# A state-space layer and a SoLU block on one Trainium2 core: one pair of accumulator banks for two products, and whole 64x64 blocks stored to memory instead of their 32x32 diagonal blocks

## The chip, the cores and the metric

The kernel runs on one core of one Trainium2 chip. The metric is the device time of one execution in microseconds (us), taken as the median of several executions. The engines are named as in the profile: PE (matmuls; PEld is its weight load), DVE (vector), ACT (activations), POOL (GpSimd) and SP (here it only issues DMAs). Every engine works through its own list of instructions in order. A "q" behind an engine's name is its sequencer.

## The reference, cut to what matters

The first part is a recurrence over 768 steps for 4 batches of 8 heads with a 40x40 state; its output, regrouped to 3072 rows of 320, goes through a feed-forward block:

```python
for t in range(S):                     # r, k, v, w, a, b: (4, 8, 768, 40)
    y[:, :, t] = einsum('bhd,bhde->bhe', r_t, state)
    Sa = einsum('bhde,bhe->bhd', state, a_t)
    state = state * w_t[:, :, None, :] - einsum('bhd,bhe->bhde', Sa, b_t) \
            + einsum('bhd,bhe->bhde', v_t, k_t)
x = y.transpose(0, 2, 1, 3).reshape(3072, 320)
h = x @ w_in                           # 320 x 1024
solu = h * softmax(h)
ln = (solu - mean(solu)) / sqrt(var(solu) + 1e-6) * g_ln
out = ln @ w_out                       # 1024 x 320
```

## The kernel before, in words

**Tiling.** The 768 steps are cut into 12 chunks of 64. A work item `i` is one chunk of one pair of batches, so there are 24 items. Within a chunk the recurrence becomes matmuls on 64x64 blocks, one for each of the 16 (batch, head) couples of the item, plus the inverse of a unit triangular 64x64 matrix for each couple. That matrix is called `nt` and is made by `norm(i)`: 16 matmuls into the accumulator tile `pnt`, and a masked copy by DVE (`masked`, line 383).

**The inverse.** The two 32x32 diagonal blocks of each `nt` are inverted column by column on DVE (`invert`, lines 427 to 451, tiles `blk`, `prod`, `uu`). DVE needs them in another layout: 128 partitions, one 32x32 block each, for two items at once (`GRP = 2`). So `norm` stores them to a DRAM tile `nt_dram`, and `spread` loads them back as `blk`, in four DMAs of 32 partitions, as soon as both items' stores have landed. The inverses go through DRAM again (`uu_dram`) and come back with `bring` as `tu` and `uh`. The off-diagonal 32x32 part is made on PE from products: `couple` (tile `py`, read by ACT into `wy`, line 481) and `close` (tile `pz`).

**Slots.** The main loop (line 827) runs over slots `i` from -1 to 27, and is a software pipeline written out by hand. In slot `i` stand, in PE's order: `solved(i)` (tile `pu`), `scores(i+1)` (`ps`), `stated(i)` (transposes of the state, `pst`; in the slots named in `THIN`, line 28, ahead of `scores`), transposes for item `i+5` (`front`, `front_b`, `decay_turned`), parts of the feed-forward block of earlier items (`hidden`, tile `h`; `output`, tile `po`, in two halves of four accumulating steps), then `couple(i+1)` (`py`), `norm(i+5)` (`pnt`), `answered(i)` (`pl`, line 591, read by DVE into `lu`), the second half of `output`, `close(i+1)` (`pz`), `read(i)` (`pyo`), `carried` and `driven` (`px`), `folded` (`plnT`), and transposes for item `i+2`. `norm(i+5)` exists up to slot 18 only, since there are 24 items; `couple(i+1)` exists up to slot 22. The first four `norm`s (items 0 to 3) stand in a loop ahead of the slots (line 771).

Between PE's pieces DVE works off the inverse in small steps (`some(n)` runs the next `n` steps; `shares`, line 825, says how many at each place of a slot). `flip(i+1)` (line 469, `tu<-tu`) is a DVE transposition that `couple(i+1)` needs.

**Accumulator banks.** The pool `ps1` gives pairs of banks with the tag `banks` and two buffers:

```python
def banks(name):
    return ps1.tile([P, 2, 512], FP32, tag="banks", name=name)
```

Each call takes the buffer of the call before the last one, and the first matmul into it waits until that earlier tile has been read. In a full slot the calls come in the order `pu`, `ps`, `py`, `pnt`, `pl`, `pz`, `pyo`, `px`, so that `pl` takes the pair of `py`.

**Queues.** `norm(i)` stores with four DMAs of 32 partitions each (line 414), all on POOL for `i > 3`; for the first four items two of the four are on SP. POOL's list has also the products `kb` (`scaled`, line 345), part of the transposed outputs (`left`, tile `xT`), the loads `raw_r`, and `blk`.

Of the kernel before, what the change touches and what calls it, by code (L numbers as in the profile page):

```python
# [9 lines left out]
FP32 = mybir.dt.float32  # L10
# [8 lines left out]
C = 64  # L19
Q = 32  # L20
IN_ROWS = (((0, 80), (240, 280), (160, 168)), ((80, 160), (280, 320), (200, 208)), ((168, 200), (208, 240)))
GRP = 2
# [29 lines left out]
def kernel(  # L52
# [18 lines left out]
    nc = tc.nc  # L71
    B, H, S, D = r.shape
# [13 lines left out]
    dram = ctx.enter_context(tc.tile_pool(name="dram", bufs=3, space=bass.MemoryType.DRAM))  # L86
# [12 lines left out]
    def c_(name):  # L99
        lo, hi = where[name]  # L100
        return cst[:, lo:hi]
# [20 lines left out]
    for x in ex_t:  # L122
# [10 lines left out]
                          in_=c_("eye_hi").unsqueeze(1).to_broadcast([P, 8, Q]))  # L133
# [5 lines left out]
    def banks(name):  # L139
        return ps1.tile([P, 2, 512], FP32, tag="banks", name=name)  # L140

    def bank(name):
        return ps3.tile([P, 512], FP32, tag="bank", name=name)
# [83 lines left out]
    def mean_part(t, lo, hi, start, stop=True):  # L227
        for c in range(lo, hi):
            nc.tensor.matmul(t[:, 0:DM], lhsT=c_("mean"), rhs=w2[:, c, :], start=start and c == lo, stop=stop and c == hi - 1)

    def mean_of(lo, hi, begun):
        t = bank("pmean")
        nc.tensor.matmul(t[:, 0:DM], lhsT=ident, rhs=begun, start=True, stop=False)
        mean_part(t, lo, hi, False)
        return mean_kept(t)

    def mean_kept(t):
        mean = two.tile([P, DM], FP32, tag="osb", name="mean", bufs=1)
        nc.scalar.copy(out=mean, in_=t[:, 0:DM])
        return mean  # L240
# [7 lines left out]
    def half(p):  # L248
        return slice(C * p, C * p + C)

    def rows(p):
        return slice(C * p, C * p + D)
# [3 lines left out]
    def in_turn(tile_of, some=units):  # L256

        lots = {}
        for u in some:
            lots.setdefault(tile_of(*u), []).append(u)  # L260
        lots = list(lots.values())
        return [lot[n] for n in range(max(map(len, lots))) for lot in lots if n < len(lot)]

    def mm(o, lhsT, rhs, start=True, stop=True):
        nc.tensor.matmul(o, lhsT=lhsT, rhs=rhs, start=start, stop=stop, skip_group_check=True)  # L265
# [3 lines left out]
    def fence():  # L269
        nc.tensor.drain()  # L270
# [8 lines left out]
    st = [dict() for _ in range(N + 16)]  # L279
    blocks, inverse = {}, {}  # L280
# [10 lines left out]
    def ok(i):  # L291
        return 0 <= i < N
# [12 lines left out]
    def load_values(i):  # L305
        if not ok(i):
            return
        d = st[i]
        d["lv"] = two.tile([P, H, W2], FP32, tag="lv", name="lv", bufs=3)
        d["raw_r"] = two.tile([P, H, D], FP32, tag="raw_r", name="raw_r")  # L310
        load(d["lv"][:, :, C:], v, i)
        load(d["raw_r"], r, i, nc.gpsimd)
# [41 lines left out]
    def tokens(name, bufs=1):  # L354
        return two.tile([P, 2, 4, C], FP32, tag=name, name=name, bufs=bufs)
# [20 lines left out]
    def front_b(i):  # L376
        if not ok(i):
            return
        d = st[i]
        d["bT"] = kept("bT", turned("b", d["kb"][:, H:]))  # L380

    def masked(dst, t):
        nc.vector.tensor_tensor(out=dst, in0=t.rearrange("p b (j c) -> p b j c", j=4),  # L383
                                in1=tri.unsqueeze(1).unsqueeze(1).to_broadcast([P, 2, 4, C]), op=ALU.mult)

    def keyed(t, u):
        p, q, g, h = u
        return t[rows(h), p, 2 * q + g]

    def valued(t, u):  # L390
        p, q, g, h = u
        return t[rows(q), p, 2 * g + h]

    def norm(i):
        if not ok(i):
            return
        d = st[i]
        t = banks("pnt")
        for u in in_turn(lambda p, q, g, h: (h, p ^ h)):
            p, q, g, h = u  # L400
            j = 2 * q + g
            mm(t[half(p ^ h), h, j * C:j * C + C], keyed(d["bT"], u), keyed(d["aT"], u))
        nt = d["nt"] = tokens("nt", AHEAD)
        masked(nt, t[:, :, 0:256])
        n, at = divmod(i, GRP)
        if at == 0:
            blocks[n] = dram.tile([2, 2 * GRP * H, Q, Q], FP32, tag="nt_dram", name="nt_dram")

        to = blocks[n].rearrange("e (a h x) s c -> a e x s h c", a=GRP, x=2)[at]
        for x in range(2):  # L410
            for e in range(2):
                home = C * x + Q * e
                queue = nc.gpsimd if i > 3 or x else nc.sync
                queue.dma_start(out=to[e, x], in_=nt[home:home + Q].rearrange("p h j c -> p (h j) c")[:, :, Q * e:Q * e + Q])  # L414

    def spread(n):
        nb = two.tile([P, Q, Q], FP32, tag="blk", name="blk")
        for y in range(2):  # L420
            for e in range(2):
                home = C * y + Q * e
                queue = nc.gpsimd if n or y else nc.sync
                queue.dma_start(out=nb[home:home + Q], in_=blocks[n][e])
        return nb

    def invert(n):
# [43 lines left out]
    def couple(i):  # L471
        if not ok(i):
            return
        d = st[i]
        t = banks("py")
        for u in in_turn(lambda p, q, g, h: (p ^ h, p)):
            p, q, g, h = u
            j = 2 * q + g
            x = half(p ^ h)
            mm(t[half(p), h, j * Q:j * Q + Q], d["nt"][x, h, j], d["tu"][x, 4 * h + j, 0:Q])  # L480
        nc.scalar.activation(out=wy[:, :, :, 0:Q], in_=t[:, :, 0:4 * Q].rearrange("p h (j c) -> p h j c", j=4),  # L481
                             func=AF.Copy, scale=c_("neg_hi"))
# [104 lines left out]
    def answered(i):  # L587
        if not ok(i):
            return
        d = st[i]  # L590
        t = banks("pl")
        for u in in_turn(lambda p, q, g, h: (q, p)):
            p, q, g, h = u
            at = (2 * g + h) * C
            mm(t[half(p), q, at:at + C], d["nuT"][rows(q), p ^ h ^ q, 2 * h + g], valued(d["rT"], u))
        masked(d["lu"].rearrange("p (q x) c -> p q x c", q=2)[:, :, :, 0:C], t[:, :, 0:256])
# [230 lines left out]
    for i in range(-1, N + 3 + LAG):  # L827
        j, m = i + AHEAD, i - LAG
        pieces = shares.get(i, (0, 5, 4, 4) if i % GRP else (3, 5, 4, 5))
        some_weights = narrowed.get(i, (0, 0, 0))  # L830
        if i >= 1:
            bring(i + 1)
        if i >= 0:
            load_values(i + 2)
        narrow(0, pieces[0])

        solved(i)
        if i in THIN:
            stated(i)
            front(j)  # L840
        if i >= 0:
            scores(i + 1)
        if i >= 0:
            load_keys(j + 3, "w")
        load_keys(j + 2, "bak")

        if i not in THIN:
            stated(i)
            front(j)
        hidden(m - 2, ((0, 1),))  # L850
        if i == 3 + LAG:
            centred(mean)
        narrow(some_weights[1], pieces[1])
        front_b(j)
        if ok(j + 2):
            logged(j + 2)
        if i == 1 + LAG:
            first = ps2.tile([P, DFF], FP32, tag="h", name="mean")
            mean_part(first, 0, 2, True, False)
        decay_turned(j + 1)  # L860
        hidden(m - 2, ((1, 1),))
        flip(i + 1)
        highest(m - 2)
        scaled(j + 1)
        left(i - 1)
        if i == 1 + LAG:
            mean_part(first, 2, 3, False)
            mean = mean_kept(first)
        decay(j + 2)
        output(m - 3, 0)  # L870

        some(pieces[2])
        if i == 2 + LAG:
            mean = mean_of(3, 6, mean)
        couple(i + 1)
        exped(m - 2)
        norm(j)
        answered(i)
        weighed(m - 2)
        spreadof(m - 2)  # L880
        if ok(j) and j % GRP == GRP - 1:
            begin_inverse(j // GRP)
        if i == 0:
            turn_g()
        output(m - 3, 1)

        close(i + 1)
        read(i, True)
        carried(i + 1)
        narrow(some_weights[2], pieces[3], ok(j) and j % GRP == GRP - 1)  # L890
        by_value(i + 2)
        if ok(m - 1):
            hidden(m - 1, ((2, 0), (2, 1)))
        fence()
        read(i, False)
        driven(i + 1)
        leave(i)
        begin_narrow(narrowed.get(i + 1, (0,))[0])
        folded(m - 2)
        hidden(m - 1, ((0, 0),))  # L900
        attend_kv(i + 2)
        hidden(m - 1, ((1, 0),))
        attend_r(i + 2)
        if i == 2 + LAG:
            mean = mean_of(6, NF, mean)
# [30 lines left out]
```

## Time and profile before

| what | value |
|---|---|
| three runs | 621.02, 621.37 and 622.67 us; median 621.37 |
| the profiled execution | 622.67 us, of which the span of instructions is 620.9 |
| PE, DVE, ACT, POOL busy | 556.5, 450.2, 265.5, 279.1 us |
| mean granted clock of PE | 0.915 |
| `nt_dram` stores | 96 DMAs of 32 KB, 88 of them on POOL |
| `blk` loads | 48 DMAs of 128 KB, 46 of them on POOL |

The table is read from the profile's page and from the list of DMA issues. Times below are places in the span, counted from its start. "Idle before" an instruction is the time that its engine stood still ahead of it, with the instruction that ended it.

### The profile page before, as it was taken

The numbers are of one execution on the slowest core, as the hardware profiler recorded it, in microseconds if no ns is written. First come the engines' busy times: TensorE is split into PE (matmuls) and PEld (weight loads), VectorE is DVE, ScalarE is ACT, GpSimd is POOL, SyncE is SP. The second block draws the span as 40 slices with busy tenths as digits, with TensorE's granted clock in tenths as the row PEclk, the third lists the DMA queues.
The fourth block names the chain that finished last, engine by engine and source line by source line (L and its number), as shares of the span: only waits on it lengthen the run. The fifth ranks groups of instructions, "written<-read, shape, count | busy, mean of one in ns | idle before, by whom it ended". The sixth has DMA issues, their size and how long they took to land.

```text
span 620.9 us, 26739 instructions
## 1 busy us (share of the span) xinstructions
PE 556.5 (90%) x11453; PEld 404.8 (65%) x11453; DVE 450.2 (73%) x1262; ACT 265.5 (43%) x548; POOL 279.1 (45%) x492
## 2 busy tenths in 40 slices
PE   4662767979899999999999999999999999999994
PEld 3442655856677777777777777777777776776553
DVE  4696896988996878869868868868687688433431
ACT  3531454546444444444454454445434343443221
POOL 3455345365635654464574456265633721322200
PEclk9555755669999999999999999999999999999998
DMA  8774867365246455454554464464522612310000
GB/s 165 123 141 99 190 125 150 85 136 117 51 71 136 76 118 99 91 110 86 93 116 86 83 130 83 95 122 75 112 47 54 111 37 45 70 36 25 26 22 21
DMA packets 211150, 56.79 MB, mean 91 GB/s; under 512 B 196176, under 2 KB 206008, under 8 KB 211032
## 3 DMA queue, kind: packets, MB, share of 16 engines
q1 hardware_dynamic: 191544, 32.99, 30.3%
q0 software_dynamic: 12784, 17.42, 12.2%
q10 hardware_dynamic: 6704, 4.67, 2.7%
q8 instruction: 90, 1.47, 1.0%
q14 instruction: 28, 0.23, 0.1%
HBM read 40.10 MB, written 10.22 MB: 81 GB/s over the span
## 4 chain that ended last, share of the span: by engine, by line
PE 70%; DVE 14%; issue 5%; DMA 4%; POOL 4%; ACT 2%; ACTq 0%; DVEq 0%; POOLq 0%; SPq 0%
PE po L735 16%; PE h L265 16%; PE pyo L265 7%; DVE uu L442 4%; DVE prod L440 4%; PE plnT L724 4%; PE pu L265 3%; PE px L265 3%; PE ps L265 3%; PE py L265 2%; PE pl L265 2%; PE pz L265 2%; PE pst L517 2%; PE pcum L333 1%; PE pk L350 1%
## 5 line engine op out<-in xcount | busy, mean ns | idle before, releaser
L265 PE MATMUL h<-w_in,xT 128*128 128x512 f32 (+1 forms) x288 | 124.3, 618 | 0.0
L414 POOL DMA_DIRECT2D nt_dram<-nt x88 | 51.9, 597 | 142.6 <-DVE nt L383 130.6
L735 PE MATMUL po<-w,lnT 128*128 128x320 f32 x384 | 112.7, 438 | 0.5 <-ACT lnT L725 0.5
L442 DVE TENSOR_TENSOR uu<-uu,prod 128x30 f32<-128x30 f32 (+4 forms) x360 | 103.6, 288 | 12.3
L440 DVE TENSOR_TENSOR prod<-blk,uu 128x30 f32<-128x30 f32 (+4 forms) x360 | 97.1, 270 | 11.0 <-DMA blk<-nt_dram 1.4
L735 PEld LDWEIGHTS po<-w,lnT 128*128 128x128 f32 x384 | 71.0, 190 | 32.7 <-issue 4.1
L383 DVE TENSOR_TENSOR psi<-ps,cst 128x512 f32<-128x512 f32 x24 | 16.6, 690 | 57.2 <-PE ps L265 57.2
L713 POOL TENSOR_TENSOR rs<-c,mhalf 128x1 f32<-128x1 f32 x24 | 13.5, 563 | 90.3 <-DVE c L712 90.3
L662 POOL DMA_DIRECT2D xT<-x x96 | 49.8, 522 | 0.0
L265 PEld LDWEIGHTS h<-w_in,xT 128*128 128x128 f32 (+1 forms) x288 | 37.6, 190 | 9.5 <-issue 8.1
L682 DVE TENSOR_REDUCE nmax<-h 128x1 f32<-128x1024 f32 x24 | 28.6, 1193 | 18.6 <-PE h L265 18.6
L265 PE MATMUL pyo<-lv,kb 64*64 64x104 f32 x768 | 38.6, 272 | 2.2
L650 POOL TENSOR_TENSOR st<-tot,ex 104x160 f32<-104x160 f32 x44 | 21.7, 508 | 38.0 <-DVE tot L646 28.0
L265 PEld LDWEIGHTS pyo<-lv,kb 64*64 64x64 f32 x768 | 24.2, 144 | 21.7 <-issue 21.5
L265 PE MATMUL pyo<-lu,kb 64*64 64x104 f32 x768 | 37.3, 265 | 0.0
L481 ACT ACTIVATE wy<-py,cst 128x256 f32<-128x256 f32 x24 | 11.4, 474 | 54.9 <-PE py L265 54.9
L566 ACT COPY x<-px 128x320 f32<-128x320 f32 x24 | 10.2, 426 | 57.3 <-PE px L265 57.3
L288 POOL DMA_DIRECT2D raw_r<-in_r_dram x48 | 34.3, 719 | 0.0
L739 ACT ACTIVATE osb<-po,rs 128x320 f32<-128x320 f32 x24 | 12.7, 528 | 48.5 <-PE po L735 32.8
L690 ACT ACTIVATE e<-h,nmax 128x1024 f32<-128x1024 f32 x24 | 26.6, 1108 | 14.3 <-DVE nmax L682 14.3
L696 DVE TENSOR_TENSOR e<-h,e 128x1024 f32<-128x1024 f32 x24 | 29.2, 1217 | 4.7 <-ACT e L690 4.7
L704 DVE BATCH_NORM_STATS2 bs<-e 128x6 f32<-128x512 f32 x48 | 30.9, 686 | 0.8
(131 smaller groups left out, 1169.5 us busy)
## 6 DMA issues: line engine op xcount, KB each, us to landing
blk<-nt_dram POOLq DMA_DIRECT2D x46, 128.0 KB, 3.5
raw_w<-in_w_dram SPq DMA_DIRECT2D x48, 80.0 KB
a<-in_a_dram SPq DMA_DIRECT2D x48, 80.0 KB
raw_r<-in_r_dram POOLq DMA_DIRECT2D x48, 80.0 KB, 2.8
lv<-in_v_dram SPq DMA_DIRECT2D x48, 80.0 KB
out_dram<-osb ACTq DMA_DIRECT2D x24, 160.0 KB
raw_b<-in_b_dram SPq DMA_DIRECT2D x44, 80.0 KB
raw_k<-in_k_dram SPq DMA_DIRECT2D x42, 80.0 KB
```

The costliest lines, as they stand in the source:

```text
L265: nc.tensor.matmul(o, lhsT=lhsT, rhs=rhs, start=start, stop=stop, skip_group_check=True)
L288: queue.dma_start(out=x[half(p), :, 0:D], in_=ap[2 * bp + p, :, ci * C:(ci + 1) * C, :].rearrange("h t d -> t h d"))
L414: queue.dma_start(out=to[e, x], in_=nt[home:home + Q].rearrange("p h j c -> p (h j) c")[:, :, Q * e:Q * e + Q])
L440: nc.vector.tensor_tensor(out=t, in0=nb[:, j:j + 1, j + 1:Q].to_broadcast([P, n_c, m]), in1=u[:, 0:n_c, j:j + 1].to_broadcast([P, n_c, m]) ...
L442: nc.vector.tensor_tensor(out=u[:, 0:n_c, j + 1:Q], in0=u[:, 0:n_c, j + 1:Q], in1=t, op=ALU.subtract)
L662: nc.gpsimd.dma_start(out=xT[to:to + Q, 2], in_=x[at + P - 3 * D:at + D, 2])
L682: nc.vector.tensor_reduce(out=nmax, in_=d["h"], axis=AX.X, op=ALU.max, negate=True)
L690: nc.scalar.activation(out=e, in_=d["h"], func=AF.Exp, bias=d["nmax"], accum_out=d["esum"])
L696: nc.vector.tensor_tensor(out=d["e"], in0=d["h"], in1=d["e"], op=ALU.mult)
L704: nc.vector.bn_stats(out=bs[:, x], in_=d["e"][:, x * 512:x * 512 + 512])
L724: nc.tensor.transpose(out=t[:, j * P:(j + 1) * P], in_=d["e"][:, f * P:(f + 1) * P], identity=ident)
L735: nc.tensor.matmul(d["out"][:, 0:DM], lhsT=d["lnT"][:, f, :], rhs=w2[:, f, :], start=f == 0, stop=f == NF - 1)
```

## The change

The tiles `py` and `pl` become one tile: the loop takes it after `pnt` and hands it to `couple(i+1)`, which uses the first 128 columns of each bank, and to `answered(i)`, which uses the 256 columns behind them. `pnt` is taken ahead of it, and given to `norm`. In a full slot there are thus seven calls of `banks` in place of eight: `pu`, `ps`, `pnt`, `py` (with `pl` in it), `pz`, `pyo`, `px`. The order of the instructions on PE stays.

`norm` stores the whole of `nt` with one DMA of 128 partitions (8 runs of 64 numbers, 256 bytes, from each) in place of four DMAs of 32 partitions (8 runs of 128 bytes from each); the DRAM tile holds 64x64 blocks. The store is on SP for the first four items, and on POOL after them. `spread` still loads `blk` with four DMAs of 32 partitions, but reads its 32x32 blocks out of the 64x64 blocks, so that what was one run of 4096 bytes for a partition is 32 runs of 128 bytes. `THIN`, which names slot 19 among the slots with the state's transposes ahead of the scores, is the same in both kernels.

```diff
-    def norm(i):
+    def norm(i, t=None):
         if not ok(i):
             return
         d = st[i]
-        t = banks("pnt")
+        if t is None:
+            t = banks("pnt")
...
         if at == 0:
-            blocks[n] = dram.tile([2, 2 * GRP * H, Q, Q], FP32, tag="nt_dram", name="nt_dram")
-
-        to = blocks[n].rearrange("e (a h x) s c -> a e x s h c", a=GRP, x=2)[at]
-        for x in range(2):
-            for e in range(2):
-                home = C * x + Q * e
-                queue = nc.gpsimd if i > 3 or x else nc.sync
-                queue.dma_start(out=to[e, x], in_=nt[home:home + Q].rearrange("p h j c -> p (h j) c")[:, :, Q * e:Q * e + Q])
+            blocks[n] = dram.tile([2 * GRP * H, C, C], FP32, tag="nt_dram", name="nt_dram")
+        queue = nc.sync if i < 4 else nc.gpsimd
+        queue.dma_start(out=blocks[n].rearrange("(a h x) s c -> a x s h c", a=GRP, x=2)[at].rearrange("x s h c -> (x s) h c"),
+                          in_=nt.rearrange("p h j c -> p (h j) c"))
...
-                queue.dma_start(out=nb[home:home + Q], in_=blocks[n][e])
+                queue.dma_start(out=nb[home:home + Q], in_=blocks[n][:, Q * e:Q * e + Q, Q * e:Q * e + Q])
...
-        t = banks("py")
+        t = d["py"]
...
-        t = banks("pl")
+        t = d["pl"][:, :, 4 * Q:]
...
         some(pieces[2])
         if i == 2 + LAG:
             mean = mean_of(3, 6, mean)
+
+        pnt = banks("pnt") if ok(j) else None
+        if ok(i) or ok(i + 1):
+            st[i]["pl"] = st[i + 1]["py"] = banks("py")
         couple(i + 1)
         exped(m - 2)
-        norm(j)
+        norm(j, pnt)
         answered(i)
```

## The prediction

> **What bounds the kernel now.** I read the page first (busy times, then the span in slices), then busy time by stretches of the span, then the order in time around the places that the change touches.
>
> ```profile
> span 620.9 us, 26739 instructions
> ...
> PE 556.5 (90%) x11453; PEld 404.8 (65%) x11453; DVE 450.2 (73%) x1262; ACT 265.5 (43%) x548; POOL 279.1 (45%) x492
> ```
>
> By stretches (length, then PE, PEld, DVE, ACT and POOL busy, PE's granted clock, DMA share, GB/s):
>
> ```profile
> 0.00:64.00 64.00, 33.48 (x288) 22.07 (x290) 42.88 (x121) 22.73 (x46) 29.38 (x52) 0.63 0.70 131
> 64.00:168.00 104.00, 83.09 (x1901) 66.11 (x1905) 89.50 (x251) 52.74 (x112) 52.35 (x88) 0.74 0.59 123
> 168.00:470.00 302.00, 299.26 (x6758) 220.30 (x6752) 238.55 (x687) 139.24 (x292) 158.49 (x280) 1.00 0.50 96
> 470.00:567.00 97.00, 95.01 (x2224) 68.52 (x2216) 60.76 (x170) 37.66 (x77) 32.76 (x64) 1.00 0.29 57
> ```
>
> From slot 4 (168 us) on PE is busy 99% of the time; a slot takes 21.5 us, and only what makes PE stand still, or gives it more to do, counts there. In the first 64 us nothing is full: that is a chain of waits between engines and DMAs. Then DVE (89.50 of 104) leads.
>
> **The banks, full slots.** Slot 12, in order of time (start, us, engine, line; idle before in brackets):
>
> ```profile
> 348.87 0.67 PE L265 MATMUL py<-tu,nt 64*64 64x32 f32 x32
> ...
> 349.61 0.47 ACT L481 ACTIVATE wy<-py,cst 128x256 f32<-128x256 f32 x1 [2.02 <-PE py L265]
> ...
> 350.13 0.56 PEld L265 LDWEIGHTS pl<-rT,nuT 40*64 40x64 f32 x32 [0.24 <-ACT wy L481]
> 350.14 0.69 PE L265 MATMUL pl<-rT,nuT 40*64 40x64 f32 x32
> ```
>
> `pl` starts 0.05 us after ACT has finished reading `py`: today because it takes `py`'s pair of banks. From slot 2 to 18 `pl` comes 1.26 us after `py` each time, with `pnt` (0.49) in between. In the changed program `pl` shares the tile with `py`, in other columns, and still waits for the same ACT instruction (the built program's list of waits names `wy` for it). So full slots neither gain nor lose: 0. The cover: `py` now waits for DVE's reading of `ps` and `pnt` for ACT's of `pu`, where it was the other way round; both readings are over some 5 us before. DVE's `lu` waits for `wy` as well, but `pl` ends after that anyway. One rule speaks of just this: the Trainium skill, page "PSUM — Partial Sum Buffer", section "PSUM bank collisions raise a hardware error", has accesses of two engines kept apart by bank and by 32 partitions, not by address, so other columns are no way out of the wait. Were the wait by address, `pl` would follow `pnt` 0.28 us sooner in 17 slots, and slots 19 to 22 would stay as they are.
>
> **The banks, slots 19 to 22.** There `pnt` is gone (no item is left), and today `pl` takes the other pair. Slot 21:
>
> ```profile
> 536.55 0.67 PE L265 MATMUL py<-tu,nt 64*64 64x32 f32 x32
> ...
> 537.04 0.67 PE L265 MATMUL pl<-rT,nuT 40*64 40x64 f32 x32
> 537.28 0.47 ACT L481 ACTIVATE wy<-py,cst 128x256 f32<-128x256 f32 x1 [3.92 <-PE py L265]
> ```
>
> `pl` starts 0.49 us after `py` and does not wait for `wy`. In the changed program the wait for `wy` stands there too, in these four slots, and nothing is between to hide it: 1.26 in place of 0.46 (slots 19 and 20) and 0.49 (21 and 22) is +0.80, +0.80, +0.77, +0.77, together **+3.1 us**. Queued behind `pl` on PE is the second half of `output`, which has no wait of its own, and so all of PE's list. Does something soak it up? In slots 19 and 20 PE waits 0.68 and 0.43 us for DVE's `flip` just before `py`; but DVE itself stood idle 4.8 and 1.9 us for PE's `ps` earlier in these slots, so its work shifts with PE's. I take all 3.1; the lower bound, if both slots soak it up, is 1.5.
>
> **The stores and loads, head of the program.** Between 13 and 17 us:
>
> ```profile
> 13.11 0.43 ACT L336 ACTIVATE inv<-h 128x320 f32<-128x320 f32 x1
> ...
> 14.66 1.38 POOL L414 DMA_DIRECT2D nt_dram<-nt  x2 [4.76 <-DVE nt L383]
> ...
> 16.05 0.88 POOL L345 TENSOR_TENSOR kb<-raw_b,inv 128x320 f32<-128x320 f32 x1
> 16.98 0.25 PEld L350 LDWEIGHTS pb<-cst,kb 128*104 128x104 f32 x2 [2.63 <-POOL kb L345]
> ```
>
> POOL's list has the two stores of item 0 ahead of `kb` of item 1, whose input `inv` is ready at 13.54; PE waits for `kb`. With the first four stores on SP alone, `kb` can start at 13.6, and `pb` when PE is through with the transposes before it, at 14.6: **-2.4 us** for `norm(1)` (nt at 20.27 now). Behind it comes the store, the load of `blk`, and the first step of the inverse, at 28.91, whose DVE work runs without a gap to 51.8 and hands on to the first slot. What the transfers add: the row that has 1024 runs of 128 bytes is `uu_dram`, 0.56 us to issue and 3.1 to 4.0 from issue to landing. The store's single DMA has 1024 runs of 256 bytes: taken like it, it lands 3.4 to 4.3 us after `nt` is done (with 0.3 for the signal), and now POOL issues its part of `blk` 3.8 us after that (24.75 against 20.97): -0.4 to +0.5, I take 0. Each of `blk`'s four DMAs goes from 32 runs to 1024. Today the first step starts 3.1 us after the last is issued (25.85). Lower bound: they overlap, and the last lands 2.5 after its issue, as `uu_dram` did at best; with POOL's two issues 0.4 longer in all (below) that is -0.2. Upper bound: they go one behind the other; queue q1 spent 30.3% of 16 engines' span on 191544 packets, 15.7 ns each, so 1024 packets over 16 engines take 1.0 us, and three more DMAs ahead of the last make +3.0. I take +1.4, about the middle, since the runs of 128 bytes were never loaded four at a time in this trace. Sum of the head: -2.4 + 0 + 1.4 = **-1.0** (from -3.0 to +1.1).
>
> The Trainium skill, page "DMA: Bandwidth & Descriptors", section "Specifications", wants transfers of at least 512 bytes for line rate and has smaller ones read, changed and written back; by it, an estimate, `blk` would take twice its 3.1 us, and the head would come out at +0.7 and not at -1.0.
>
> **The stores and loads, slots.**
>
> ```profile
> L414 POOL DMA_DIRECT2D nt_dram<-nt x88 | 51.9, 597 | 142.6 <-DVE nt L383 130.6
> ...
> blk<-nt_dram POOLq DMA_DIRECT2D x46, 128.0 KB, 3.5
> ```
>
> A store's four issues of 0.60 become one. Its price for 1024 runs is not in the trace on POOL: 256 runs cost 0.60 and 512 (`raw_r`) 0.72, so between 0.72 and, drawn on in a line, 0.96. That frees 1.4 to 1.7 us of POOL a slot; the four `blk` issues cost 0.2 to 0.45 each more than their 0.51, in every second slot. POOL is busy 45% of the span and stands idle before each `nt` store, so from slot 4 on both are worth 0; before it, where in slot 1 POOL runs without a pause from 87.6 to 94.6, ±0.5, taken as 0. The later landing of `blk` is covered: in the ten groups loaded in slots the last part lands 1.7 to 6.1 us ahead of DVE's first use, except the last group, 0.5 ahead of `uu` and 1.0 ahead of the first `prod` (494.18 and 495.19). `flip` has another 0.9 us of slack against PE in full slots. If the cover of the last group goes, what is late is `flip` in slot 19, and PE with it, one for one.
>
> **Sum.** +3.1 - 1.0 = +2.1 us. The profiled execution took 622.67 (1.8 beyond its span) and would become 624.8; it lies 1.3 above the median 621.37, which becomes **623.5**. Own range of this case, with the tail at 3.1 and the head from -2.4 to +1.1: 622.1 to 625.6. A measurement of this kernel can tell some 0.3%, 1.9 us, from no change.
>
> **Rivals.** *The head pays for the tail* (not slower): the transfers cost nothing more, and PE, less idle at the head, also runs faster there (`pb` after the wait takes 1.09 against 0.65 for the transposes before it, `pnt` 1.13 against 0.97), so that `norm(1)` comes 3.4 us sooner, and another 0.8 is saved at POOL in slots -1 to 3: 3.1 - 4.2 = -1.1, 620.3. It decides from the point where the first step of the inverse starts before 25.8 (3.1 sooner). For it: PE's 2.63 us wait for POOL is plain. Against it: DMA engines are 70% busy in that stretch, and the new transfers are in finer pieces.
>
> *The loads come late* (slower by more): `blk`'s pieces go one behind the other, +3.0. The head becomes +0.6, the last group, with 1.0 of cover, +2.0, the tail +3.1: +5.7, 627.1. For it: the count of packets for `blk` grows 32-fold. Against it: `uu_dram` with as many for each DMA lands in 3.1.
>
> *The wait is not felt* is a rival as well: the tail counts 1.5 and not 3.1; I put it into the first rival's chance, since it ends near 620.3 to 622 with any head below zero.
>
> **How the numbers follow.** The forecast has 0.47 (0.32 of it beyond 0.3% slower, 0.15 within), the first rival 0.27 (0.10 faster, 0.17 within), the late loads 0.26 (all slower). Faster 0.10, same 0.32, slower 0.58. The range leaves out the best tenth of the first rival and the worst of the late loads: 620.0 to 627.5.
>
> **What would show it.** In the profile after: `pl`'s matmuls (under the name `py`) 1.26 us behind `py` in slots 19 to 22, with idle time before them put down to ACT's `wy`; slots 5 to 18 at 21.5 us as before; no stores on POOL before `kb` at 13.6; the first `prod` near 27.9; 22 stores on POOL. I am wrong about the tail if `pl` follows at 0.5, about the head if `prod` starts outside 26 to 30, about the slots if DVE's `uu<-blk` has idle time before it put down to `blk`.

## The result, and the profile after

The changed kernel takes 622.60 us (median), the kernel before 619.89 us in the same set of runs: a ratio of 1.0050, with a 95% interval of 1.0031 to 1.0069, so 0.5% slower (2.7 us between the medians). On the median of 621.37 that the forecast started from this is 624.5, where 623.5 was forecast. The profiled execution of before (622.67 us) was the slowest of the 20 that were taken of it in the end, 2.8 us above their median; so the two profiles, 622.67 and 623.49 us, lie only 0.8 us apart, and that difference must be read together with the medians.

From the page of after: span, busy times, the two groups that the change touches, TensorE's queue of instruction fetches (packets, MB, share of 16 engines) and, last, the landing times:

```profile
span 621.7 us, 26680 instructions
...
PE 556.6 (90%) x11453; PEld 404.9 (65%) x11453; DVE 450.3 (72%) x1262; ACT 265.5 (43%) x548; POOL 259.0 (42%) x424
...
q8 instruction: 90, 1.47, 1.0%
...
L410 POOL DMA_DIRECT2D nt_dram<-nt x20 | 18.8, 940 | 121.0 <-DVE nt L383 99.9
...
L421 POOL DMA_DIRECT2D blk<-nt_dram x46 | 36.9, 809 | 12.3 <-issue 6.6
...
blk<-nt_dram POOLq DMA_DIRECT2D x46, 128.0 KB, 4.7
nt_dram<-nt POOLq DMA_DIRECT2D x20, 256.0 KB, 3.7
```

POOL has 20 us less to do (259.0 against 279.1), as the change says: 20 stores of 940 ns in place of 88 of 597, and loads of 809 ns. PE has the same work. The queue `q8`, which the page of before has with the same numbers, plays a part below that the prediction left out.

The same stretches as before (length, then PE, PEld, DVE, ACT and POOL busy, PE's granted clock, DMA share, GB/s):

```profile
0.00:64.00 64.00, 35.08 (x412) 24.52 (x413) 45.17 (x132) 25.40 (x52) 25.74 (x44) 0.66 0.82 149
64.00:164.00 100.00, 79.83 (x1785) 63.07 (x1783) 87.43 (x239) 50.08 (x106) 48.23 (x73) 0.75 0.66 128
164.00:467.00 303.00, 300.03 (x6730) 220.56 (x6725) 238.53 (x688) 138.94 (x291) 146.10 (x238) 1.00 0.53 101
467.00:567.00 100.00, 95.44 (x2208) 68.61 (x2204) 60.67 (x170) 37.90 (x77) 32.27 (x60) 1.00 0.29 57
```

Slot 4 begins 4 us sooner; from there the full slots take a microsecond more, and the last slots three and a half more. In the head the DMA engines are busy 82% of the time and not 70%.

**The tail.** In order of time, PE and ACT in slots 19 to 22 (start, us, engine, line; idle before in brackets). The shared tile bears the name `py`, so `pl`'s matmuls are those with `rT,nuT`:

```profile
496.82 0.69 PE L265 MATMUL py<-rT,nuT 40*64 40x64 f32 x32 [0.58 <-ACT wy L478]
...
517.02 0.69 PE L265 MATMUL py<-rT,nuT 40*64 40x64 f32 x32 [0.58 <-ACT wy L478]
...
535.46 0.67 PE L265 MATMUL py<-tu,nt 64*64 64x32 f32 x32
...
536.20 0.47 ACT L478 ACTIVATE wy<-py,cst 128x256 f32<-128x256 f32 x1 [3.92 <-PE py L265]
...
536.72 0.69 PE L265 MATMUL py<-rT,nuT 40*64 40x64 f32 x32 [0.59 <-ACT wy L478]
...
556.43 0.69 PE L265 MATMUL py<-rT,nuT 40*64 40x64 f32 x32 [0.59 <-ACT wy L478]
```

`pl` starts 1.26 us behind `py` in slot 21, and 0.05 us after `wy` ends (536.67). The four distances are 1.25, 1.25, 1.26 and 1.26, against 0.46, 0.46, 0.49 and 0.49 before: +3.14 us, as forecast, and each of the four waits is put down to ACT's `wy`.

**The head, up to the first step of the inverse.** Before:

```profile
16.98 1.09 PE L350 MATMUL pb<-cst,kb 128*104 128x128 f32 x4 [2.38 <-POOL kb L345]
...
20.27 0.69 DVE L383 TENSOR_TENSOR nt<-pnt,cst 128x512 f32<-128x512 f32 x1 [4.76 <-PE pnt L265]
...
24.75 1.09 POOL L424 DMA_DIRECT2D blk<-nt_dram  x2 [0.49 <-issue]
...
28.00 0.41 DVE L434 TENSOR_SCALAR uu<-blk 64x512 f32<-64x512 f32 x1
...
28.91 0.19 DVE L440 TENSOR_TENSOR prod<-blk,uu 128x30 f32<-128x30 f32 x1 [0.35 <-DMA blk<-nt_dram]
```

After:

```profile
13.57 0.88 POOL L345 TENSOR_TENSOR kb<-raw_b,inv 128x320 f32<-128x320 f32 x1 [3.71 <-ACT inv L336]
...
14.61 1.30 SPq L410 DMA_DIRECT2D nt_dram<-nt  x1
...
15.22 0.62 PE L350 MATMUL pb<-cst,kb 128*104 128x128 f32 x4 [0.33 <-ACT ex L366]
...
17.33 0.69 DVE L383 TENSOR_TENSOR nt<-pnt,cst 128x512 f32<-128x512 f32 x1 [1.53 <-PE pnt L265]
...
22.29 1.78 POOL L421 DMA_DIRECT2D blk<-nt_dram  x2 [2.86 <-DMA nt_dram<-nt]
...
25.71 0.42 DVE L431 TENSOR_SCALAR uu<-blk 64x512 f32<-64x512 f32 x1 [1.00 <-DMA blk<-nt_dram]
...
28.11 0.19 DVE L437 TENSOR_TENSOR prod<-blk,uu 128x30 f32<-128x30 f32 x1 [1.83 <-DMA blk<-nt_dram]
```

`kb` runs at 13.57, no store ahead of it; `pb` comes at 15.22 and not at 16.98; the first `prod` comes at 28.11 and not at 28.91. Forecast were 13.6, 14.6 and 27.9. The first `uu`, which reads only the 64 partitions that SP loads, comes 2.3 sooner; `prod` then waits 1.83 us for POOL's half.

**The head, after the inverse: not forecast.** The two halves of the first `uu_dram` store, and the load of `tu` behind them. Before:

```profile
51.99 0.56 ACTq L448 DMA_DIRECT2D uu_dram<-uu  x1
...
55.99 0.56 SPq L448 DMA_DIRECT2D uu_dram<-uu  x1
...
59.18 0.38 ACTq L461 DMA_DIRECT2D tu<-uu_dram  x1
```

After:

```profile
51.20 0.55 SPq L445 DMA_DIRECT2D uu_dram<-uu  x1
...
51.20 0.59 ACTq L445 DMA_DIRECT2D uu_dram<-uu  x1
...
54.98 0.35 ACTq L458 DMA_DIRECT2D tu<-uu_dram  x1
```

Both halves are ready at the same time, and before, SP's went out 4.0 us after ACT's. The chain that ended last, before, has the landing of ACT's half ahead of SP's (start, us):

```profile
51.99 3.94 DMA uu_dram<-uu
...
55.99 3.11 DMA uu_dram<-uu
```

The reason is in how the program tells that a DMA has landed. A landing is added to a count (a semaphore); in the traces the DMAs of SP and ACT take eight such counts in turn, 101 to 108, and in the program of before both halves have 108, so that SP's half waits until ACT's has landed. The change issues fewer DMAs at the head, the turns fall otherwise, the two halves have 104 and 106, and `py` of slot -1 starts at 59.62 in place of 63.86: 4.24 sooner, 0.8 of them from the inverse's earlier start and 3.4 from this.

**The full slots: not forecast.** From the starts of `pu`, slots 5, 6, 7 and 12 take 22.31, 21.80, 21.71 and 21.97 us, where before they took 21.88, 21.52, 21.53 and 21.53. The two largest pieces, in slots 5 and 12, lie in the middle of a group of equal matmuls; that of slot 5, in order of time on PE:

```profile
187.68 0.45 PE L265 MATMUL ps<-rT,vT 40*64 40x64 f32 x17
188.31 0.46 PE L265 MATMUL ps<-rT,vT 40*64 40x64 f32 x15 [0.17 <-issue]
```

After 17 matmuls PE stands still (0.39 us between two starts, where 15 ns are usual on average), and nothing in the profile releases it. Against before, the account of the two profiles is: start of slot 4 -4.14, slots 4 to 18 +1.13, slots 19 to 22 +3.52 (of them the four waits 3.14), rest +0.30; sum +0.81.

### The profile page after: what moved, and what is told of

Same layout as the page of the kernel before. It is cut to its first block, busy times and chain, and to the rows that moved or that the text cites. A ratio compares the mean times of both kernels' runs of the same rounds, so it can differ in the third digit from the quotient of the medians.

```text
span 621.7 us, 26680 instructions
## 1 busy us (share of the span) xinstructions
PE 556.6 (90%) x11453; PEld 404.9 (65%) x11453; DVE 450.3 (72%) x1262; ACT 265.5 (43%) x548; POOL 259.0 (42%) x424
## 3 DMA queue, kind: packets, MB, share of 16 engines
q8 instruction: 90, 1.47, 1.0%
## 4 chain that ended last, share of the span: by engine, by line
PE 70%; DVE 15%; DMA 5%; ACT 3%; issue 3%; SPq 2%; ACTq 0%; POOL 0%; DVEq 0%; POOLq 0%
PE po L732 16%; PE h L265 15%; PE pyo L265 7%; DVE uu L439 5%; PE py L265 4%; PE pu L265 4%; PE plnT L721 3%; DVE prod L437 3%; PE px L265 3%; PE ps L265 3%; PE pz L265 2%; DMA uu_dram<-uu 2%; PE pst L514 2%; PE pr L350 2%; PE pk L350 1%
## 5 line engine op out<-in xcount | busy, mean ns | idle before, releaser
L439 DVE TENSOR_TENSOR uu<-uu,prod 128x30 f32<-128x30 f32 (+4 forms) x360 | 105.9, 294 | 12.4
L437 DVE TENSOR_TENSOR prod<-blk,uu 128x30 f32<-128x30 f32 (+4 forms) x360 | 95.1, 264 | 11.4 <-DMA blk<-nt_dram 1.8
L410 POOL DMA_DIRECT2D nt_dram<-nt x20 | 18.8, 940 | 121.0 <-DVE nt L383 99.9
L421 POOL DMA_DIRECT2D blk<-nt_dram x46 | 36.9, 809 | 12.3 <-issue 6.6
```

The source lines that it names most:

```text
L410: queue.dma_start(out=blocks[n].rearrange("(a h x) s c -> a x s h c", a=GRP, x=2)[at].rearrange("x s h c -> (x s) h c"), in_=nt.rearrange( ...
L421: queue.dma_start(out=nb[home:home + Q], in_=blocks[n][:, Q * e:Q * e + Q, Q * e:Q * e + Q])
L437: nc.vector.tensor_tensor(out=t, in0=nb[:, j:j + 1, j + 1:Q].to_broadcast([P, n_c, m]), in1=u[:, 0:n_c, j:j + 1].to_broadcast([P, n_c, m]) ...
L439: nc.vector.tensor_tensor(out=u[:, 0:n_c, j + 1:Q], in0=u[:, 0:n_c, j + 1:Q], in1=t, op=ALU.subtract)
```

## The experiments

Each was timed beside the kernel before on its chip, except that the changed kernel has its own set of runs (above). Times are places in each kernel's one profile; slots 4 to 18 and slots 19 to 22 are each given as a whole, from the starts of `pu`. The pairs of numbers in brackets behind a gain in us are its 95% interval.

| kernel | ratio to before, 95% interval | slot 4 starts | slots 4 to 18 | slots 19 to 22 |
|---|---|---|---|---|
| before | 1 | 167.51 | 323.04 | 76.03 |
| the changed kernel | 1.0050 [1.0031, 1.0069] | 163.37 | 324.17 | 79.55 |
| 1 shared pair alone | 1.0039 [1.0023, 1.0054] | 165.59 | 323.23 | 79.27 |
| 2 stores and loads alone | 0.9995 [0.9976, 1.0014] | 161.64 | 324.40 | 76.41 |
| 3 first `uu_dram` store on SP | 0.9975 [0.9958, 0.9992] | 161.66 | 322.98 | 76.14 |
| 4 changed, own pair at the tail | 0.9983 [0.9958, 1.0007] | 161.38 | 324.12 | 76.61 |
| 5 whole stores at the head only | 0.9931 [0.9912, 0.9951] | 162.75 | 322.62 | 75.91 |
| 6 strided loads, no whole store in slots | 0.9963 [0.9946, 0.9980] | 159.52 | 322.88 | 76.26 |
| 7 changed, PE's list shifted by 128 | 1.0115 [1.0086, 1.0143] | 163.87 | 326.28 | 80.53 |
| 8 changed, slots' transfers as before | 1.0005 [0.9984, 1.0027] | 161.26 | 323.38 | 79.18 |
| 9 first stores on SP, nothing else | 1.0038 [1.0019, 1.0058] | 166.02 | 323.04 | 75.91 |
| 10 as 9, and 3 | 0.9941 [0.9920, 0.9962] | 160.08 | 322.73 | 76.30 |

The stretch of slots 4 to 18 parts the twelve profiles: 324.12 to 326.28 us in the four that have whole stores there (the changed kernel, 2, 4 and 7), 322.62 to 323.38 in the eight that have not. Single slots do not part them so well: kernels 1 and 9, with the slots' stores of before, take 21.79 and 21.80 us in slot 6, so its 21.80 in the changed kernel is no mark of the change.

**1. The shared pair alone**, on the kernel before:

```diff
...
-        t = banks("pl")
+        t = d["pl"][:, :, 4 * Q:]
...
+        if ok(i) or ok(i + 1):
+            st[i]["pl"] = st[i + 1]["py"] = banks("py")
...
```

> The kernel before with the shared tile alone (stores and loads of the inverse's blocks as before). Theory (the wait for wy in slots 19 to 22 is most of the loss): 3.1 us slower than before, py to pl 1.26 us in these four slots and the same 1.26 in slots 2 to 18, head as before. Rival (the shared tile is free, the loss of the changed kernel comes from the finer transfers): within 1 us of before.

Measured: 1.0039, which on 620.77 us is +2.4 (1.4 to 3.4). `pl` follows `py` by 1.25 to 1.26 us in slots 19 to 22 and stays at 1.26 in the full slots, which take 0.2 us more in all. So nearly all of the slowdown that the change shows (2.7) comes with the shared pair, and by the trace it lies in the tail.

**2. The stores and loads alone**, on the kernel before:

```diff
...
-        for x in range(2):
-            for e in range(2):
-                home = C * x + Q * e
-                queue = nc.gpsimd if i > 3 or x else nc.sync
-                queue.dma_start(out=to[e, x], in_=nt[home:home + Q].rearrange("p h j c -> p (h j) c")[:, :, Q * e:Q * e + Q])
+        queue = nc.sync if i < 4 else nc.gpsimd
+        queue.dma_start(out=blocks[n].rearrange("(a h x) s c -> a x s h c", a=GRP, x=2)[at].rearrange("x s h c -> (x s) h c"),
+                          in_=nt.rearrange("p h j c -> p (h j) c"))
...
-                queue.dma_start(out=nb[home:home + Q], in_=blocks[n][e])
+                queue.dma_start(out=nb[home:home + Q], in_=blocks[n][:, Q * e:Q * e + Q, Q * e:Q * e + Q])
```

> The kernel before with the whole-block stores and the loads out of 64x64 blocks alone (py and pl in pairs of their own). Theory: the head comes out sooner, since the two halves of uu_dram of the first group get different DMA semaphores and are issued within 0.1 us (51.99 and 55.99 before), and the full slots lose some 1.5 to 2 us; in all about 0.4 us faster than before (from 2 faster to 1 slower). Rival (the loss comes from the transfers): 2.7 us slower than before.

Measured: 0.9995, -0.3 us (-1.5 to +0.9). Here too the halves of `uu_dram` go out together (49.91), and slots 5, 6, 7, 12 and 15 take 22.03, 21.83, 21.91, 21.91 and 22.44: a gain at the head and a loss in the full slots, about equal.

**3. Both halves of the first `uu_dram` store on SP**, on the kernel before; by the list of waits they then have different counts:

```diff
-            queue = nc.sync if n or not y else nc.scalar
+            queue = nc.sync
             queue.dma_start(out=inverse[n][:, y::2], in_=u[C * y:C * y + C])
```

> The kernel before with both halves of the first group's uu_dram store issued on SP, where they get different DMA semaphores, and not one on ACT and one on SP with the same semaphore. Theory (SP's half waits 4 us for the landing of ACT's half): the second is issued 0.6 us after the first, the first slot's py starts about 3 us sooner than its 63.9, the time is 2 to 3 us below before. Rival (the transfers would be as late anyway, or something else is late next): py of the first slot near 63.9, time within 1 us of before.

Measured: 0.9975, -1.6 us (-2.6 to -0.5), less than expected. The halves go out at 50.24 and 50.92, `tu` is loaded at 55.74, `py` of slot -1 starts at 60.36. That is 2.5 us sooner than in kernel 1 (62.85), which has the shared count, and 3.5 sooner than in the profile of before, but part of it comes from ahead of the store, whose first half goes out 0.95 and 1.75 sooner. From the first half to `py` it is 10.12 us here, against 11.66 in kernel 1 and 11.87 before: so the count is worth 1.5 to 1.8 here, as the median says. In the changed kernel, where the two halves go out on two queues at once, the same stretch is 8.42.

**4. The changed kernel, with a pair of its own for `pl` in slots 19 to 22:**

```diff
-            st[i]["pl"] = st[i + 1]["py"] = banks("py")
+            st[i + 1]["py"] = banks("py")
+            st[i]["pl"] = st[i + 1]["py"] if ok(j) or not ok(i + 1) else banks("pl")
```

> The changed kernel, but where norm has no item left (slots 19 to 22) pl takes a pair of banks of its own. Theory: py to pl back to 0.46 to 0.49 us in these four slots, 3.1 us below the changed kernel, so about 0.4 us below before. Rival (the wait is not felt at the end): as the changed kernel, 2.7 us above before.

In order of time on PE, slot 21 of this kernel:

```profile
532.08 0.67 PE L265 MATMUL py<-tu,nt 64*64 64x32 f32 x32
532.56 0.65 PE L265 MATMUL pl<-rT,nuT 40*64 40x64 f32 x29
```

Measured: `pl` is back at 0.48 behind `py`, slots 19 to 22 lose 2.9 us, the ratio is 0.9983. With the pair shared in the full slots and not at the tail, the change costs nothing that this measurement tells. So the two experiments, one part done and one part undone, agree on the tail.

**5. Whole stores and strided loads for the first four items only**, every product in its own pair; from item 4 on the packed tile and the four diagonal stores of before (kernel 2 with this edit):

```diff
-        queue = nc.sync if i < 4 else nc.gpsimd
...
+        if i < 4:
+            nc.sync.dma_start(out=blocks[n].rearrange("(a h x) s c -> a x s h c", a=GRP, x=2)[at].rearrange("x s h c -> (x s) h c"),
+                              in_=nt.rearrange("p h j c -> p (h j) c"))
+        else:
+            to = blocks[n].rearrange("e (a h x) s c -> a e x s h c", a=GRP, x=2)[at]
+            for x in range(2):
+                for e in range(2):
+                    home = C * x + Q * e
+                    nc.gpsimd.dma_start(out=to[e, x], in_=nt[home:home + Q].rearrange("p h j c -> p (h j) c")[:, :, Q * e:Q * e + Q])
...
-                queue.dma_start(out=nb[home:home + Q], in_=blocks[n][:, Q * e:Q * e + Q, Q * e:Q * e + Q])
+                src = blocks[n][:, Q * e:Q * e + Q, Q * e:Q * e + Q] if n < 2 else blocks[n][e]
+                queue.dma_start(out=nb[home:home + Q], in_=src)
```

> The kernel before, with the whole store and the strided loads only for the first four items (two groups, all before the full slots); from item 4 on the stores are the four diagonal ones into a packed tile, and the loads are plain, as before; every product has its own pair of banks. The change's gain at the head without its cost in the full slots, if my reading is right. Theory A (PE's pauses inside a group of matmuls in slots 5, 6, 7, 12 and 15 come from the stores and loads of those slots): these slots are back at 21.9, 21.5, 21.5, 21.5 and 21.9 us, slot 4 starts near 161.6 us as with the store changed alone, the stretch from the start of slot 4 to that of slot 19 is 323.0 us in place of 324.2 to 324.4, and the time is 0.9965 of before (617.5 to 618.5 beside 620). Rival B (the pauses come from the head's being earlier, and so from where the slots lie): the stretch stays at 324.2 to 324.4, and the ratio at 0.9995.

Measured: 615.71 us, 0.9931; slots 5, 6, 7, 12 and 15 take 21.94, 21.52, 21.52, 21.52 and 21.85. The pauses go with the slots' transfers, and not with where the slots lie in time. The gain is larger than expected: 4.3 us in place of 2.2.

**6. Strided loads in the slots, without whole stores there:** kernel 2, but from item 4 on four diagonal stores into the 64x64 blocks.

```diff
-        queue = nc.sync if i < 4 else nc.gpsimd
...
+        else:
+            to = blocks[n].rearrange("(a h x) s c -> a x s h c", a=GRP, x=2)[at]
+            for x in range(2):
+                for e in range(2):
+                    home = C * x + Q * e
+                    nc.gpsimd.dma_start(out=to[x, Q * e:Q * e + Q, :, Q * e:Q * e + Q], in_=nt[home:home + Q].rearrange("p h j c -> p (h j) c")[:, :, Q * e:Q * e + Q])
```

> As the store-and-load part of the change alone, but from item 4 on each item is stored by its four diagonal pieces into the 64x64 blocks, so that only the loads of blk are strided there and the whole stores are gone from the full slots. In the trace of the changed kernel the pauses in slots 7 and 12 fall while a whole store is in flight, and that in slot 5 just after the loads of blk. Theory A expects slots 7 and 12 back at 21.5, slot 5 still 0.1 to 0.4 above 21.88, the stretch from slot 4 to slot 19 at 323.2 to 323.6, and a ratio of 0.997 to 0.998. If the loads make all of it, the stretch is 324.2 as in the change and the ratio 0.9995; if the stores make all of it, the stretch is 323.0.

Measured: slots 4 to 18 take 322.88 us, slots 5, 7 and 12 are 21.88, 21.52 and 21.52, and only slot 15 (22.17) is long. So in these profiles the whole stores make nearly all of it, and the strided loads some 0.3 us at most. The times of the runs say otherwise: 6 is 2.0 us slower than 5, and 2 is 2.0 slower than 6, each with an uncertainty of some 1.6, so by them the strided loads cost as much as the whole stores. How the cost divides stays open.

**7. The changed kernel, with 128 more PE instructions at the head:**

```diff
-        for u in in_turn(lambda p, q, g, h: (h, p ^ h)):
+        for u in in_turn(lambda p, q, g, h: (h, p ^ h)) * (3 if i == 0 else 1):
```

> The changed kernel, with the first item's norm multiplied three times over instead of once (the same products again, 128 more TensorE instructions at the head, about 1.0 us more there). In the changed kernel and four of the other runs every pause of over 0.2 us inside a group of matmuls falls on an instruction whose place in TensorE's list is 193 or 194 above a multiple of 256, and 16 KB are fetched once for each 256 instructions by the queue of kind instruction, last 1.2 to 1.8 us before the pause ends. Theory F (TensorE stands still because the next 256 instructions have not come yet, their fetch being held up by the store's or the loads' packets): with 128 more instructions ahead the pauses of 188.3 (scores) and 354.5 (output) are gone from these groups; where pauses stand, they are again at 193 or 194 above a multiple of 256 (with a shift of one or two at most), so in other groups or in the other half of a slot; the sum over the full slots may come out shorter or longer by up to 1.4 us. Rival G (the matmuls themselves are held up by the transfers in flight): the pauses stay in the same groups of slots 5, 7 and 12, whatever the place in the list, and the stretch from slot 4 to slot 19 stays at 324.2.

On PE, in order of time:

```profile
360.85 0.27 PE L350 MATMUL pa<-cst,a 128*104 128x128 f32 x1
362.49 0.54 PE L350 MATMUL pa<-cst,a 128*104 128x128 f32 x3 [1.37 <-issue]
...
448.35 0.39 PE L265 MATMUL ps<-rT,vT 40*64 40x64 f32 x11
449.98 0.57 PE L265 MATMUL ps<-rT,vT 40*64 40x64 f32 x21 [1.24 <-issue]
```

Measured: slots 5, 6, 7 and 12 are clean (21.88, 21.52, 21.52, 21.52), and the pauses stand elsewhere: 1.5 us in the transposes of `a` in slot 13, 0.4 in `pyo` of slot 14, 1.5 in `ps` of slot 17. Counted in PE's list, they fall on instructions 13506, 15042 and 17345: 194, 194 and 193 above a multiple of 256, as in the changed kernel (5570 and 12994: 194 and 194). In the twelve profiles of this study there are 18 pauses of over 0.2 us inside a group of equal matmuls (those of the feed-forward block left out), after the first 60 us, and all 18 fall at 193 or 194. So PE pauses where its next block of 256 instructions begins, and not where a certain matmul meets a transfer. The kernel lost 3.8 us to the changed one by the medians (626.44 against 622.60, in two sets of runs), 1.0 of it the expected cost at the head (in the profile slot 4 begins 0.5 later). So what the pauses cost changes with where the 256-blocks fall in a slot. Twelve of the 18 pauses stand in the four kernels with whole stores in the slots, but three, of 0.2 to 0.4 us, stand in kernels 1, 3 and 10, which have the slots' stores and loads of before: a whole store is not needed for a pause.

**8. The changed kernel, with the slots' stores and loads as before** (the edit of experiment 5 on the changed kernel).

> The changed kernel, shared pair and all, but from item 4 on the stores are the four diagonal ones into a packed tile and the loads are plain, so that only its slots' transfers are undone. Theory (the pauses in the full slots come from the whole stores in flight, mostly): the stretch from the start of slot 4 to that of slot 19 is 322.8 to 323.2 us in place of 324.17, with slots 5, 6, 7 and 12 at 21.9, 21.5, 21.5 and 21.5; slots 19 to 22 still have the couplings 1.25 us after what the solve gives; the time is 1.2 to 2.0 below the changed kernel's, a ratio of 1.001 to 1.003 to before, and 3 above the version with the same stores and separate pairs (0.9931). Rival: the shared pair has a part in the pauses; then the stretch stays near 324.2 and the ratio near 1.005.

Measured: 1.0005; slots 6, 7 and 12 are back at 21.52, 21.53 and 21.52, but slot 5 takes 22.49, with a pause of 0.56 us in `ps`, on instruction 5570 again. So the pair of banks has no part in the pauses of slots 7 and 12, and the one in slot 5 comes without a whole store too: there the fetch of the block started at 183.87, 2.5 us after PE had entered the block before it, while the plain loads of `blk` were in flight (issued 178.9 to 181.6, a part of them landed at 186.05). Against kernel 5, which differs by the shared pair alone, it is 4.6 us slower, 3.3 of them in slots 19 to 22 of the profile.

**9. The first four items' stores on SP, nothing else**, on the kernel before:

```diff
-                queue = nc.gpsimd if i > 3 or x else nc.sync
+                queue = nc.gpsimd if i > 3 else nc.sync
```

> The kernel before with one word changed: the first four items' stores all go out on SP (four diagonal ones each), the packed tile and plain loads stay. It takes POOL's two stores out of the way of kb without finer loads. My step at the head had -2.4 for that and +1.4 for the finer loads: by it, the first prod comes near 26.5 us (28.91 before, 28.0 with the strided loads). In this program's list of waits SP's third store of item 3 waits on the completion count that ACT's half of the first uu_dram store adds to, and SP's half stands behind it. Theory S (a shared count serializes the two): ACT's half goes out near 50, SP's some 4 us later, and what the solve gives of slot -1 comes near 61.5 and not near 58; ratio 0.995 to 0.998. Rival (the 4 us of before were an accident of that queue's load): both halves go out within 1 us, py near 58, ratio 0.991.

SP's and ACT's queues, in order of time:

```profile
50.86 0.56 ACTq L448 DMA_DIRECT2D uu_dram<-uu  x1
```

```profile
38.57 15.75 SPq L414 DMA_DIRECT2D nt_dram<-nt  x8
54.43 1.28 SPq L288 DMA_DIRECT2D raw_w<-in_w_dram  x2
56.22 0.55 SPq L448 DMA_DIRECT2D uu_dram<-uu  x1
...
59.99 0.31 SPq L461 DMA_DIRECT2D tu<-uu_dram  x1
```

Measured: 1.0038, slower than before. SP's eight stores take 15.75 us, because the third store of item 3 (issued at 53.52) waits for the count that ACT's half of `uu_dram` adds to; SP's half stands behind it and goes out 5.4 us after ACT's. `py` of slot -1 starts at 65.01; 61.5 was expected. And the first `prod` comes at 28.29, not at 26.5: with plain loads it is no sooner than with strided ones.

**10. The same with both halves on SP** (the edit of experiment 3 added).

> The same, with both halves of the first uu_dram store on SP, so that, by the program's list of waits, neither stands behind a count that the other adds to. Theory S: halves 0.7 us apart near 50, first load of tu near 54.5, what the solve gives of slot -1 near 59, full slots as before (stretch 322.6 to 323.1), ratio 0.990 to 0.994, some 2 to 3 us below the kernel with the one word changed. Rival: no difference between the two.

```profile
49.82 1.27 SPq L448 DMA_DIRECT2D uu_dram<-uu  x2
51.14 1.68 SPq L288 DMA_DIRECT2D lv<-in_v_dram  x2
54.14 0.31 SPq L461 DMA_DIRECT2D tu<-uu_dram  x1
```

Measured: 0.9941; `py` of slot -1 at 58.83. From the one line that moves the second half from ACT's queue to SP's come 5.7 us of the median (616.93 against 622.64, on the same chip). That is the shared count shown by taking it away, for the second time. Over all twelve profiles the stretch from the first half's issue to `py` of slot -1 is 11.7 to 14.2 us in the three kernels in which SP waits for ACT's half (before, 1 and 9), and 8.4 to 10.1 in the nine others. Kernels 5 and 10 beat both kernels of this case, by 4.3 and 3.7 us against before.

## Why the prediction was right, and where it was not

**The tail, +3.1: right, in mechanism and size.** 3.14 us in the four distances, and by the medians +2.4 (1.4 to 3.4) when done alone. The rival that it would not be felt (1.5 in place of 3.1) falls by the traces: slots 19 and 20 soaked up nothing, and slot 19 even has 0.48 more, since PE waits 1.15 us for DVE's `flip` there and not 0.68. The rule that was weighed, of the Trainium skill, page "PSUM — Partial Sum Buffer", section "PSUM bank collisions raise a hardware error", agrees with these rows: other columns of the same pair were no way out of the wait, 0.58 to 0.59 us idle in each of four slots, and `pl` at 1.26 in the full slots as before. The rows show that the program keeps the wait, not what the chip would do without it.

**The full slots, 0: wrong.** The step that failed is "so from slot 4 on both are worth 0". Its two covers held: POOL had time, and DVE never waited for `blk` in a slot. The sum left out another user of the DMA engines, PE's own instruction list. The trace has 90 fetches of 16 KB (1.47 MB in 90 packets), one for each 256 of PE's 23147 instructions. In slot 12 of before, the fetch for the block that begins in `pyo` started 1.04 us after PE had entered the block ahead of it; after the change, with a whole store in flight, 1.64 us, and at the block's first instruction PE stood still for 0.31 us. No block of a full slot, in any of these profiles, was begun less than 1.2 us after its fetch had ended. The size is +1.1 us by the two profiles. By the medians it is more: kernel 8 undoes it for -2.8, and kernels 2 and 5 differ by 4.0, each with an uncertainty of some 1.8. What lies between 1.1 and these is open; a profile shows one execution, and experiment 7 shows that one pause can be 1.5 us. That the fetch starts later because of the stores' packets is argued from the twelve stretches and from these rows; no experiment held up a fetch alone.

**The head, -1.0: about right for what it described, but with a wrong reason for one term, and the smaller part of what happened.** The first `prod` came 0.8 sooner. By the two profiles the terms are: `nt` of item 1 comes 2.9 sooner (17.33 against 20.27; forecast 2.4), POOL's first `blk` issue 0.5 later behind it (forecast 0), and the first `prod` 1.7 later behind that issue (forecast 1.4). The first term is shown: in all nine kernels that take POOL's stores away from `kb`, `nt` starts at 15.95 to 17.57, and in the three that do not, at 18.80 to 20.27. It is larger than forecast since `pb` and `pnt` behind it also run faster (0.62 and 0.69 us in place of 1.09 and 1.13), which only the first rival had counted. The third term has its size, but not its reason, the finer pieces. From the start of the last `blk` issue to the first `prod` it is 3.2 to 3.6 us in the three kernels with the stores of before, 4.6 to 5.2 in the seven with strided loads, and 4.9 and 4.4 in kernels 9 and 10, whose loads are plain: these pay most of it too. Kernels 2, 5 and 6 have the same head and their first `prod` differs by 1.6 us (26.39 to 28.02), so one profile cannot size a term of 1 us here. What the nine share is that they load sooner; that the earlier loads meet fuller DMA engines (82% against 70% in the head of the changed kernel) fits, but it was not isolated. The estimate that was set beside this step, drawn from the Trainium skill, page "DMA: Bandwidth & Descriptors", section "Specifications" (line rate from 512 bytes on), would have doubled the load's time; from issue to landing POOL's loads went from 3.5 to 4.7 us as a median over all of them, so the trace shows a third more, and at the head no doubling.

**What the head's sum missed** is the gain of 3.4 us in the first `uu_dram` store. No wait of `norm` or `spread` showed it; it stood in the profile of before as 4.0 us between two halves of one store, ready together, on two queues. The prediction went through every queue that a store was moved past, and did not ask what removing DMAs does to the counts of those behind them.

**Why the total was near all the same.** Luck had a part: two misses of opposite sign lay between the right terms. By the profiles: -0.8 for the first inverse, -3.4 for the shared count, +1.1 in the full slots, +3.5 in the last ones, +0.3: +0.8. Some 1.9 us of the gain at the head seem to belong to the profiled execution of before and not to the change, since kernel 1, whose stores and loads are those of before, begins slot 4 at 165.59 and not at 167.51; with that the sum is +2.7, and the medians give +2.7. **The rivals:** "the head pays for the tail" named the right place (the head did begin slot 4 four us sooner in the profile) but not the cause; its point of decision, the first step before 25.8, was not reached, and the gain that came by another way was partly eaten by the full slots. "The loads come late" fell: DVE's last group did not wait for `blk` (the last landing that the profile tells is at 488.75, the first use at 491.62). Small misses: 20 stores on POOL and not 22 (24 items less four); the own range of 622.1 to 625.6 took the head from -2.4, where its sum had -3.0, which gives 621.5; a store's price of 0.94 us on POOL lay at the upper end of 0.72 to 0.96.

## What to carry to other kernels

Sharing a pair of banks between two products cost 0.8 us a slot where nothing stood between them (slots 19 to 22), and nothing where another product did (slots 5 to 18); so look at the slots where the pipeline runs dry, not at the full ones. Before transfers in a PE-bound stretch are called free, ask who else uses the DMA engines: a PE that idled inside a group of equal matmuls, with no releaser, stood in all 18 cases at the start of a new block of its own instructions. And when DMAs are added or taken away, look at the list of waits for which later DMAs then share a count across two queues: here the one line that parts such a pair was worth 5.7 us (kernels 9 and 10), more than the change cost.

## What the hardware showed that was not expected

- PE's instructions come by DMA, 16 KB for 256 of them, about every 5.7 us in the full slots (53 fetches in 303 us), each taking 0.9 to 1.6 us over the twelve profiles. All 18 pauses, with 0.2 to 1.6 us between two starts, fall where such a block begins.
- Two DMAs on different queues that share a completion count went one after the other: 4.0 us between two halves that were ready together (51.99 and 55.99), 5.4 us in experiment 9, and 5.7 us of the median for the one line that parts them.
- The price of issuing a DMA on POOL grew slowly with its pieces: 0.60 us for a store of 256 runs, 0.94 for one of 1024 runs; 0.51 for a `blk` load of 32 runs, 0.81 for one of 1024.
